# Token rows stored as they stand and gathered by quarters, q loaded two tokens to a partition, early gathers for two experts, the first weights loaded last

## The chip, the cores and the metric

The kernel runs on one core of one Trainium2 chip. The metric is device time in microseconds (us). Before the change three runs took 552.61, 552.60 and 547.84 us, so the median is 552.6 us. All line numbers below (L364 and so on) are those of the kernel before, unless the text says "after".

## The reference, cut to what matters

Two blocks follow each other: a retention layer (batch 4, 8 heads, 768 tokens, head width 64) and a mixture of experts over its output (3072 tokens of width 512, 8 experts, hidden width 1024, one expert for each token).

```python
for t in range(S):                      # retention, gamma per head
    state = gamma * state + einsum('bhd,bhe->bhde', k[:, :, t], v[:, :, t])
    y[:, :, t] = scale * einsum('bhd,bhde->bhe', q[:, :, t], state)
x = y.transpose(0, 2, 1, 3).reshape(B * S, H * D)          # 3072 x 512
logits = x @ w_gate
expert_idx = argmax(logits, axis=1)
gate_w = softmax(logits)[arange(N), expert_idx]
...
for e in range(E):
    h = maximum(x_sorted[lo:hi] @ w1[e], 0.0)
    y_sorted[lo:hi] = h @ w2[e]
out = gate_w[:, None] * y_sorted[inv_perm]
```

## The kernel before, in words

**Retention.** A chunk is 128 tokens of one batch; there are 6 chunks c times 4 batches b, so 24 steps n, in the order c outer, b inner. `load(n)` has SP fetch k, q and v of a step (256 KB each, rows of 64 floats), five steps ahead (`AHEAD`). `scale(n)` multiplies q and v by tables of decay powers on POOL. `transpose(n)` has PE turn k and q to heads-first form in PSUM and ACT copy them out (`kT`, L299, and `qT`, L300). `retain(n)` makes the scores (L311), masks them on DVE (`am`, L313), updates the state (L322, L325), and sums y (L335, L340), which ACT copies to `xTg` (L342). `to_rows` turns that into token rows `xg` on DVE (L347).

**Routing.** After the four batches of a chunk, `place(c)` runs in pieces, one at each `step()` of the following chunk, on all engines in an order written out by hand (`tc.manual_schedule`). It makes the logits, has ACT store `xg` in the DRAM tensor `x_d` (four DMAs, L364), finds expert, gate and rank of each token, stores the gate as column 513 of the row in `x_d` (L400), and adds the chunk's tokens to the table `inv` (slot to token) by the matmul `found` (L433). `tables` turns `inv` into row numbers: `src` to gather from `x_d`, `dst` to scatter to the output. SP is left to a scheduler; the DMAs of SP and ACT share eight completion semaphores in turn, and each waits for the DMA that had its semaphore before it.

**Experts.** Expert 0 begins early: at c = 4 `tables(inv[:, :, 0:HALF], "_e")` (L438) names its first 256 tokens, POOL gathers them (L159, one indirect DMA for 128 rows of 2052 bytes), and `layer1`/`layer2` run them between the pieces of the last `place`. Then `tables(inv)` (L507), the gathers of the rest, `turn` (gathered rows to features on partitions, 16 transposes of 32 partitions each, L191), and one `job` for each expert: 64 or fewer matmul groups of `layer1` (L200), then `layer2` (L212), gated on ACT (L218), scattered by POOL (L222). After job e POOL scatters its rows, and gathers those of e+2 (`rows_of`) while job e+1 runs; SP loads the weights of e+2 (L150, L151).

The lines of the indirect gather and of the store, which the change rewrites:

```python
R = DM + 1
x_d = dram.tile([N, R], F32, tag="x_d", name="x_d")
...
    nc.scalar.dma_start(x_d[ts(c, B * P), ts(g, P)].rearrange("(t l) r -> l t r", l=L),
                        xg[c % 2][ts(g, L), :, :, :].rearrange("p b q r -> p (b q) r"))
```

Of the kernel before, what the change touches and what calls it, by code (L numbers as in the profile page):

```python
# [20 lines left out]
P = 128  # L21


NC = 6


def decay_table(H, D):

    gamma = 1.0 - 2.0 ** (-5.0 - np.arange(H, dtype=np.float64))
    e = np.arange(1, P + 1, dtype=np.float64)[:, None]
    on = [gamma ** (e + P * c) / math.sqrt(D) for c in range(NC)]
    back = [gamma ** -(e + P * c) for c in range(NC)]
    return np.concatenate(on + back, 1).astype(np.float32)
# [15 lines left out]
def kernel(  # L53
# [39 lines left out]
    R = DM + 1  # L93
    x_d = dram.tile([N, R], F32, tag="x_d", name="x_d")

# [34 lines left out]
    tok2 = rt([P, NT, 2], "tok2", BF16)  # L130
# [3 lines left out]
    nc.gpsimd.iota(tok2[:, :, 0], pattern=[[1, NT]], base=1, channel_multiplier=0, **exact)  # L134
    nc.gpsimd.iota(tok2[:, :, 1], pattern=[[0, NT]], base=0, channel_multiplier=1, **exact)
# [3 lines left out]
    inv = rt([P, 2, E * TC], "inv")  # L139
# [15 lines left out]
    xs2 = [first.tile([P, TC, R], F32, tag=f"xs{i}", name=f"xs{i}") for i in range(2)]  # L155

    def gather(xs, idx, tiles, rows=N):
        for t in tiles:
            nc.gpsimd.indirect_dma_start(  # L159
                out=xs[:, t, :], out_offset=None, in_=x_d[0:rows, :],  # L160
                in_offset=bass.IndirectOffsetOnAxis(ap=idx[:, t : t + 1], axis=0), bounds_check=rows - 1,
                oob_is_err=False)

    def tables(got, name):

        m = got.shape[2]
        tok, none, far = (rt([P, m], f"{nm}{name}") for nm in ("tok", "none", "far"))
        src = rt([P, m], f"src{name}", U32)  # L170
        nc.vector.tensor_scalar(out=none, in0=got[:, 0, :], scalar1=1.0, scalar2=float(FAR), op0=ALU.is_lt,
                                op1=ALU.mult)
        nc.vector.scalar_tensor_tensor(out=tok, in0=got[:, 0, :], scalar=float(P), in1=got[:, 1, :], op0=ALU.mult,
                                       op1=ALU.add)
        nc.vector.scalar_tensor_tensor(out=src, in0=tok, scalar=-float(P), in1=none, op0=ALU.add, op1=ALU.add)
        tile_i, bt, ct = (rt([P, m], f"{nm}{name}", I32) for nm in ("tile_i", "bt", "ct"))
        dst = rt([P, m], f"dst{name}", U32)
        nc.vector.tensor_scalar(out=tile_i, in0=got[:, 0, :], scalar1=-1.0, scalar2=None, op0=ALU.add)  # L178
        nc.vector.tensor_single_scalar(bt, tile_i, B - 1, op=ALU.bitwise_and)
        nc.vector.tensor_single_scalar(ct, tile_i, B.bit_length() - 1, op=ALU.arith_shift_right)  # L180
        nc.vector.tensor_tensor(out=far, in0=got[:, 1, :], in1=none, op=ALU.add)
        nc.vector.scalar_tensor_tensor(out=far, in0=ct, scalar=float(P), in1=far, op0=ALU.mult, op1=ALU.add)
        nc.vector.scalar_tensor_tensor(out=dst, in0=bt, scalar=float(P * NC), in1=far, op0=ALU.mult, op1=ALU.add)
        return src, dst

    def turn(xs, xT, gate, tiles):

        nc.vector.tensor_copy(gate, xs[:, 0:tiles, DM])  # L188
        for r in range(Q):
            for g in range(Q):  # L190
                nc.vector.transpose(  # L191
                    xT[ts(g, L), :, 0 : tiles * P].rearrange("p a (t r i) -> p r t a i", r=Q, i=L)[:, r, :, :, :],
                    xs[ts(r, L), 0:tiles, ts(g, P)].rearrange("p t (a i) -> p t a i", i=L))
# [68 lines left out]
    with ExitStack() as actx:  # L262
# [5 lines left out]
        steps = [(c, b) for c in range(NC) for b in range(B)]  # L268
        qkv, scaled, front, state = {}, {}, {}, {}

        def load(n):
            c, b = steps[n]
            got = {}
            for nm, src in (("k", k), ("q", q), ("v", v)):
                got[nm] = att.tile([P, H, D], F32, tag=nm, name=nm, bufs=6)
                nc.sync.dma_start(got[nm], src[b, :, ts(c, P), :].rearrange("h t d -> t h d"))
            qkv[n] = got["q"], got["k"], got["v"]
# [7 lines left out]
        def scale(n):  # L285
            c, b = steps[n]
            qt, kt, vt = qkv.pop(n)
            mul = nc.gpsimd if n else nc.vector
            qs = att.tile([P, H, D], F32, tag="qs", name="qs", bufs=3)
            vs = att.tile([P, H, D], F32, tag="vs", name="vs", bufs=4)  # L290
            mul.tensor_tensor(out=qs, in0=qt, in1=inner(dec[:, ts(c, H)], D), op=ALU.mult)  # L291
            mul.tensor_tensor(out=vs, in0=vt, in1=inner(dec[:, ts(NC + c, H)], D), op=ALU.mult)  # L292
            scaled[n] = (qs, kt, vs)

        def transpose(n):
            qs, kt, vs = scaled.pop(n)
            qT = att.tile([P, HP, P], F32, tag="qT", name="qT")
            kT = att.tile([P, HP, P], F32, tag="kT", name="kT")
            nc.scalar.copy(out=kT, in_=heads_first(kt))  # L299
            nc.scalar.copy(out=qT, in_=heads_first(qs))  # L300
            front[n] = (kt, vs, qT, kT)

        def retain(n, then, between):
# [38 lines left out]
            nc.scalar.copy(out=xTg[c % 2][:, :, b, :], in_=y)  # L342

        def to_rows(n):

            c, b = steps[n]
            nc.vector.transpose(xg[c % 2][:, b, :, :].rearrange("p r (a l) -> p a r l", l=L),  # L347
                                xTg[c % 2][:, :, b, :].rearrange("p a (r l) -> p a r l", l=L))
# [3 lines left out]
        def place(c):  # L352
# [10 lines left out]
            for g in range(Q):  # L363
                nc.scalar.dma_start(x_d[ts(c, B * P), ts(g, P)].rearrange("(t l) r -> l t r", l=L),  # L364
                                    xg[c % 2][ts(g, L), :, :, :].rearrange("p b q r -> p (b q) r"))
# [33 lines left out]
            with nc.allow_non_contiguous_dma(reason="one gate a row"):  # L399
                nc.scalar.dma_start(x_d[ts(c, B * P), DM : DM + 1].rearrange("(b p) r -> p (b r)", p=P), gate)  # L400
# [17 lines left out]
            if c < NC - 1:  # L418
                yield
                yield  # L420
            val = att.tile([P, B, 2, E * TC], BF16, tag="val", name="val")
            at_f = at[:, :, :, :].rearrange("p b e t -> p b (e t)")
            nc.vector.tensor_tensor(out=val, op=ALU.mult, in1=inner(tok2[:, g0 : g0 + B, :], E * TC), in0=bass.AP(
                tensor=at_f.tensor, offset=at_f.offset,
                ap=[list(at_f.ap[0]), list(at_f.ap[1]), [0, 2], list(at_f.ap[2])]))
# [5 lines left out]
            found = ps("tr", 3, "found")[:, 0 : 2 * E * TC]  # L431
# [5 lines left out]
            if c == NC - 2:  # L437
                early.append(tables(inv[:, :, 0:HALF], "_e"))  # L438
                gather(xs2[0], early[0][0], range(HALF), (c + 1) * B * P)

                tot = ps("tr", 3, "tot")[:, 0:1]
                nc.tensor.matmul(tot, lhsT=ones_b, rhs=acc[:, c + 1, 0:1], start=True, stop=True)
                pad = att.tile([P, 1], F32, tag="pad", name="pad")
                nc.vector.scalar_tensor_tensor(out=pad, in0=row2, scalar=float(EARLY), in1=tot, op0=ALU.add,
                                               op1=ALU.subtract)
                nc.vector.tensor_scalar(out=pad, in0=pad, scalar1=0.0, scalar2=2.0, op0=ALU.max, op1=ALU.min)
                nc.vector.tensor_tensor(out=acc[:, c + 1, 0:1], in0=acc[:, c + 1, 0:1], in1=pad, op=ALU.add)
# [13 lines left out]
        for n in range(len(steps)):  # L461
            if n + AHEAD < len(steps):
                load(n + AHEAD)
            if n == 17:
# [18 lines left out]
            if steps[n][1] == B - 1:  # L483
                rest = place(steps[n][0])
        to_rows(len(steps) - 1)

        xe = keep.tile([P, HALF, DM], F32, tag="xe", name="xe")
        gates = [rt([P, HALF], "gate_e"), rt([P, TC - HALF], "gate_0")]
        for t in range(HALF):
            nc.vector.tensor_copy(xe[:, t, :].rearrange("p (a q l) -> p q a l", q=Q, l=L),  # L490
                                  xs2[0][:, t, 0:DM].rearrange("p (q a l) -> p q a l", q=Q, l=L))
        nc.vector.tensor_copy(gates[0], xs2[0][:, 0:HALF, DM])
# [3 lines left out]
        for t in range(HALF):  # L496
            tr = ps("tr", 3, "tre").rearrange("p (a t) -> p a t", a=DT)
            for dt in range(DT):
                nc.tensor.transpose(tr[:, dt, :], xe[:, t, ts(dt, P)], ident)
            nc.vector.tensor_copy(xTa[:, :, ts(t, P)], tr)  # L500
# [6 lines left out]
        src, dst = tables(inv, "")  # L507
        cols = [(src[:, ts(e, TC)], dst[:, ts(e, TC)]) for e in range(E)]

        cols[0] = tuple(t[:, HALF:] for t in cols[0])  # L510
        gather(xs2[1], cols[0][0], range(TC - HALF))
        turn(xs2[1], xTa, gates[1], TC - HALF)
        layer2(EARLY, hTa, wa[1], oa, 0, gates[0])
        which = regs(0)
        tc.switch_hint(which, arms_of(0), label="job0")
        layer2(EARLY, hTa, wa[1], oa, 1, gates[0])
# [10 lines left out]
    def job(e, n, xT, gate, hT, nxt):  # L527
# [5 lines left out]
        for t in [tiles - 1] + list(range(tiles - 1)):  # L533
            if e + 1 < E and t == max(tiles - 2, 0):
                tc.switch_hint({g: nxt[g] for g in (PE, ACT)}, arms_of(e + 1), label=f"job{e + 1}")
            layer2(n, hT, w2t, o2[e % 2], t, gate)
# [3 lines left out]
    def rows_of(e):  # L540

        xT = mp.tile([P, DT, W], F32, tag="xTs", name="xTs")
        xs = xs2[(e + 1) % 2]
        gather(xs, cols[e][0], range(TC))
# [115 lines left out]
```

## Time and profile before

The profiled execution took 544.2 us, of which its span is 542.5 us; the median of the three runs shown is 552.6 us.

| stretch of the span, us | what runs | PE busy in it, us |
|---|---|---|
| 0 to 16 | first loads and first step | 9.3 |
| 16 to 40 | chunk 0, start of chunk 1 | 23.8 |
| 40 to 108 | chunks 1 to 3 | 44.0 |
| 108 to 163 | chunks 3 to 5 | 53.2 |
| 163 to 205 | early half of expert 0, routing of chunk 5 | see below |
| 205 to 532 | eight expert jobs | 100% in all windows of 220 to 500 |

| engine | busy us, share of the span |
|---|---|
| PE | 490.7, 90% |
| DVE | 175.1, 32% |
| POOL | 119.0, 22% |
| ACT | 102.8, 19% |

Read the table of stretches first: the experts leave PE no idle time, the retention stage leaves it about 33 us in 163. DMA transfers are not engine work; the profile gives their bytes in each slice.

### The profile page before, as it was taken

The numbers are of one execution on the slowest core, as the hardware profiler recorded it, in microseconds if no ns is written. First come the engines' busy times: TensorE is split into PE (matmuls) and PEld (weight loads), VectorE is DVE, ScalarE is ACT, GpSimd is POOL, SyncE is SP. The second block draws the span as 40 slices with busy tenths as digits, with TensorE's granted clock in tenths as the row PEclk, the third lists the DMA queues.
The fourth block names the chain that finished last, engine by engine and source line by source line (L and its number), as shares of the span: only waits on it lengthen the run. The fifth ranks groups of instructions, "written<-read, shape, count | busy, mean of one in ns | idle before, by whom it ended". The sixth has DMA issues, their size and how long they took to land. (4 is left out here: it accounts for less than half of the span.)

```text
span 542.5 us, 7653 instructions
## 1 busy us (share of the span) xinstructions
PE 490.7 (90%) x3008; PEld 299.1 (55%) x3008; DVE 175.1 (32%) x405; ACT 102.8 (19%) x204; POOL 119.0 (22%) x135
## 2 busy tenths in 40 slices
PE   5997479299997978999999999999999999999991
PEld 4886368288774737555455455456455545445540
DVE  2565154246572549061025008003404300700000
ACT  2423022123331111022122021112002211111210
POOL 4825313033210050400230050023032004002010
PEclk9998869599997997999999999999999999999996
DMA  9999999999353691910660480075083057001010
GB/s 188 203 170 204 191 198 197 254 245 165 52 66 55 113 343 24 330 46 2 213 222 1 152 274 0 2 255 186 2 278 141 2 186 255 2 4 57 4 40 22
DMA packets 109143, 72.47 MB, mean 134 GB/s; under 512 B 81402, under 2 KB 93690, under 8 KB 109056
## 3 DMA queue, kind: packets, MB, share of 16 engines
q1 hardware_dynamic: 87952, 52.45, 39.5%
q10 hardware_dynamic: 15984, 6.35, 7.7%
q0 software_dynamic: 5120, 12.61, 6.2%
q8 instruction: 42, 0.69, 0.5%
q14 instruction: 45, 0.37, 0.2%
HBM read 60.90 MB, written 14.69 MB: 139 GB/s over the span
## 5 line engine op out<-in xcount | busy, mean ns | idle before, releaser
L212 PE MATMUL ye<-w2t,hT 128*128 128x512 f32 (+3 forms) x640 | 164.0, 455 | 0.0
L200 PE MATMUL hp<-xTs,w1t 128*128 128x416 f32 (+3 forms) x448 | 154.2, 505 | 0.0
L200 PEld LDWEIGHTS hp<-xTs,w1t 128*128 128x128 f32 x448 | 85.1, 190 | 69.1 <-issue 54.6
L212 PEld LDWEIGHTS ye<-w2t,hT 128*128 128x128 f32 (+3 forms) x640 | 74.9, 155 | 86.5 <-issue 85.0
L222 POOL DMA_INDIRECT out_dram<-o,dst x30 | 29.9, 996 | 269.0 <-ACT o L218 236.6
L191 DVE STREAM_TRANSPOSE xTs<-xs 32x512 f32<-32x512 f32 x112 | 78.7, 702 | 1.4
L188 DVE COPY gates<-xs 128x4 f32<-128x4 f32 x7 | 1.2, 170 | 185.4 <-DMA xs<-x_d,src 185.4
L202 ACT ACTIVATE hT<-hp 128x416 f32<-128x416 f32 (+4 forms) x64 | 29.4, 482 | 136.3 <-PE hp L200 93.1
L313 DVE TENSOR_TENSOR am<-sc,causal 128x512 f32<-128x512 f32 x48 | 30.8, 683 | 35.1 <-PE sc L311 32.2
L159 POOL DMA_INDIRECT xs<-x_d,src x30 | 30.3, 1011 | 37.3 <-DVE tile_i L178 28.4
L218 ACT ACTIVATE o<-ye,gates 128x512 f32<-128x512 f32 (+1 forms) x21 | 14.5, 689 | 125.5 <-PE ye L212 125.5
L322 PE MATMUL new<-vs,k 128*64 128x64 f32 x320 | 15.5, 247 | 21.8 <-ACT kT L299 21.8
L292 POOL TENSOR_TENSOR vs<-v,dec 128x512 f32<-128x512 f32 x23 | 24.1, 1048 | 48.3 <-PE y L340 38.2
L311 PE MATMUL sc<-qT,kT 64*128 64x128 f32 x384 | 29.4, 295 | 4.3 <-ACT qT L300 4.3
L291 POOL TENSOR_TENSOR qs<-q,dec 128x512 f32<-128x512 f32 x23 | 24.0, 1042 | 40.2 <-DMA q<-in_q_dram 23.3
L200 PE MATMUL hp<-xTa,w1t 128*128 128x256 f32 (+1 forms) x128 | 26.5, 373 | 6.2 <-DVE xTa L191 4.8
L342 ACT COPY xTg<-y 128x512 f32<-128x512 f32 x24 | 14.1, 588 | 84.7 <-PE y L340 35.6
L311 PEld LDWEIGHTS sc<-qT,kT 64*128 64x128 f32 x384 | 24.7, 197 | 8.2 <-ACT qT L300 5.2
L340 PE MATMUL y<-am,vs 128*64 128x128 f32 x384 | 29.2, 292 | 0.0
L200 PEld LDWEIGHTS hp<-xTa,w1t 128*128 128x128 f32 x128 | 22.2, 224 | 10.9 <-issue 7.3
L322 PEld LDWEIGHTS new<-vs,k 128*64 128x64 f32 x320 | 12.5, 154 | 27.4 <-ACT kT L299 22.6
L340 PEld LDWEIGHTS y<-am,vs 128*64 128x64 f32 x384 | 22.7, 145 | 4.1 <-issue 2.4
(121 smaller groups left out, 282.3 us busy)
## 6 DMA issues: line engine op xcount, KB each, us to landing
w1t<-in_moe_w_dram SPq DMA_DIRECT2D x8, 2048.0 KB, 9.3
w2t<-in_moe_w_dram SPq DMA_DIRECT2D x8, 2048.0 KB
k<-in_k_dram SPq DMA_DIRECT2D x24, 256.0 KB, 6.0
q<-in_q_dram SPq DMA_DIRECT2D x24, 256.0 KB, 6.4
v<-in_v_dram SPq DMA_DIRECT2D x24, 256.0 KB, 6.6
x_d<-xg ACTq DMA_DIRECT2D x24, 256.0 KB, 8.9
xs<-x_d,src POOLq DMA_INDIRECT x30
out_dram<-o,dst POOLq DMA_INDIRECT x30
```

What stands on the lines that cost most here:

```text
L159: nc.gpsimd.indirect_dma_start(out=xs[:, t, :], out_offset=None, in_=x_d[0:rows, :], in_offset=bass.IndirectOffsetOnAxis(ap=idx[:, t : t + ...
L191: nc.vector.transpose(xT[ts(g, L), :, 0 : tiles * P].rearrange("p a (t r i) -> p r t a i", r=Q, i=L)[:, r, :, :, :], xs[ts(r, L), 0:tiles, ...
L200: nc.tensor.matmul(hp, lhsT=w1t[:, 0, dt, ts(f, P)], rhs=xT[:, dt, 0:n], start=(dt == 0), stop=(dt == DT - 1))
L202: nc.scalar.activation(out=hT[:, f, 0:n], in_=hp, func=AF.Relu)
L212: nc.tensor.matmul(y[j * m : j * m + m, 0:c], lhsT=hT[:, f, t * P : t * P + m], rhs=w2t[:, 0, f, ts(j, c)], start=(f == 0), stop=(f == FT ...
L222: done = nc.gpsimd.indirect_dma_start(out=out[:, :], out_offset=bass.IndirectOffsetOnAxis(ap=idx[:, t : t + 1], axis=0), in_=o[:, t, :], i ...
L291: mul.tensor_tensor(out=qs, in0=qt, in1=inner(dec[:, ts(c, H)], D), op=ALU.mult)
L292: mul.tensor_tensor(out=vs, in0=vt, in1=inner(dec[:, ts(NC + c, H)], D), op=ALU.mult)
L311: nc.tensor.matmul(sc[j][:, a, :], lhsT=kT[r, a, :], rhs=qT[r, a, :], start=True, stop=True)
L313: nc.vector.tensor_tensor(out=am[j], in0=sc[j], in1=middle(causal[:, :], HP), op=ALU.mult)
L322: nc.tensor.matmul(new[ts(j, D), a, :], lhsT=kt[:, h, :], rhs=vs[:, h, :], start=True, stop=True)
L340: nc.tensor.matmul(y[ts(j, D), a, :], lhsT=vs[:, 2 * a + j, :], rhs=am[j][:, a, :], start=(c == 0), stop=True, skip_group_check=True)
```

## The change

1. **Layout of x_d.** It becomes 12288 rows of 128 floats (a quarter of a token each), and each chunk group is stored in one DMA of 1 MB, partition after partition, as `xg` stands. The gate is stored no more: it travels through `inv` as three bf16 parts, so `inv`, `val` and `found` have 5 planes for 2.
2. **Gather.** An indirect DMA now fetches the four quarters of 32 tokens (128 rows of 512 bytes), so an expert takes 16 for 4. `tables` spreads the token numbers over the quarters with four small matmuls (`ip`, with the constant `wrap`). `turn` becomes 4 transposes of 128 partitions.
3. **Order of steps.** Steps run in pairs of chunks: for each pair m, for each batch, the two chunks. q is loaded once for a pair, two tokens to a partition (512-byte rows), scaled and transposed in the even step; `qT` interleaves the tokens again. A group for `place` is four consecutive steps, thus 2 batches by 2 chunks.
4. **Early gathers** for experts 0 and 1 (256 tokens each); the early compute stays with expert 0, and no `xe` copies or transposes on PE are made for it.
5. **First weights.** They are asked for at n = 19, no longer at n = 17.

```diff
-    x_d = dram.tile([N, R], F32, tag="x_d", name="x_d")
+    x_d = dram.tile([N * Q, DT * L], F32, tag="x_d", name="x_d")
...
+        hl = rt([P, 2, m], f"hl{name}", BF16)
+        nc.vector.tensor_copy(hl, got[:, 0:2, :])
+        ip = ps("tr", 3, "ip")[:, 0 : Q * 2 * m].rearrange("p (g i m) -> p g i m", g=Q, i=2)
+        for g in range(Q):
+            nc.tensor.matmul(ip[:, g, :, :].rearrange("p i m -> p (i m)"), lhsT=wrap[:, g, :],
+                             rhs=hl[:, :, :].rearrange("p i m -> p (i m)"), start=True, stop=True)
...
+    def turn(xs, xT, b0, b1):
+
+        for dt in range(DT):
+            nc.vector.transpose(xT[:, dt, :], xs[:, b0:b1, ts(dt, L)])
...
-        steps = [(c, b) for c in range(NC) for b in range(B)]
+        steps = [(2 * m + e, b) for m in range(NC // 2) for b in range(B) for e in range(2)]
...
+                elif c % 2 == 0:
+                    got[nm] = att.tile([P, H, 2 * D], F32, tag=nm, name=nm, bufs=3)
+                    nc.sync.dma_start(got[nm], src[b, :, ts(c // 2, 2 * P), :].rearrange("h (t e) d -> t h (e d)", e=2))
...
+                qT2[b] = att.tile([P, HP, P, 2], F32, tag="qT", name="qT")
+                for e in range(2):
+                    nc.scalar.copy(out=qT2[b][:, :, :, e], in_=heads_first(qs[:, e, :, :]))
...
-            for g in range(Q):
-                nc.scalar.dma_start(x_d[ts(c, B * P), ts(g, P)].rearrange("(t l) r -> l t r", l=L),
-                                    xg[c % 2][ts(g, L), :, :, :].rearrange("p b q r -> p (b q) r"))
+            nc.scalar.dma_start(x_d[ts(c, B * P * Q), :].rearrange("(p r) d -> p r d", p=P),
+                                xg[c % 2][:, :, :, :].rearrange("p b r d -> p (b r) d"))
...
-                nc.scalar.dma_start(x_d[ts(c, B * P), DM : DM + 1].rearrange("(b p) r -> p (b r)", p=P), gate)
...
+            part = gate
+            for i in range(2, 5):
+                nc.vector.tensor_copy(told[:, g0 : g0 + B, i], part)
+                if i < 4:
+                    less = att.tile([P, B], F32, tag="less", name="less", bufs=3)
+                    nc.vector.tensor_tensor(out=less, in0=part, in1=told[:, g0 : g0 + B, i], op=ALU.subtract)
+                    part = less
...
-                gather(xs2[0], early[0][0], range(HALF), (c + 1) * B * P)
+                for e in range(2):
+                    gather(xs2[e], early[0][0][:, e * TC * Q :],
+                           range(HALF * Q), (c + 1) * B * P * Q)
...
-            if n == 17:
+            if n == len(steps) - AHEAD:
                 wa = weights(first, 0)
...
-        for t in range(HALF):
-            tr = ps("tr", 3, "tre").rearrange("p (a t) -> p a t", a=DT)
-            for dt in range(DT):
-                nc.tensor.transpose(tr[:, dt, :], xe[:, t, ts(dt, P)], ident)
-            nc.vector.tensor_copy(xTa[:, :, ts(t, P)], tr)
+        turn(xs2[0], xTa, 0, HALF * Q)
...
+        for e in range(2):
+            gather(xs2[e], cols[e][0], range(HALF * Q, TC * Q))
+        turn(xs2[0], xTa, HALF * Q, TC * Q)
```

## The prediction

> **What bounds the kernel now.** I began with the slices of the page, to see which stage leaves PE idle.
>
> ```profile
> PE   5997479299997978999999999999999999999991
> DMA  9999999999353691910660480075083057001010
> GB/s 188 203 170 204 191 198 197 254 245 165 52 66 55 113 343 24 330 46 2 213 222 1 152 274 0 2 255 186 2 278 141 2 186 255 2 4 57 4 40 22
> ```
>
> From slice 16 on PE is full: the experts are bound by PE, and nothing there gets shorter, as the change leaves their matmuls alone. The first 12 slices (163 us) have holes in PE while DMA is full. The table by stretches says where (length, then busy us of PE, PEld, DVE, ACT, POOL, granted clock, DMA share, GB/s):
>
> ```profile
> 40.00:48.00 8.00, 5.10 (x64) 4.44 (x60) 3.86 (x9) 2.58 (x5) 3.27 (x3) 0.88 0.91 176
> 60.00:72.00 12.00, 1.50 (x26) 1.38 (x24) 1.34 (x5) 1.68 (x4) 3.12 (x3) 0.63 1.13 183
> 92.00:108.00 16.00, 5.60 (x69) 5.17 (x67) 3.78 (x15) 1.68 (x4) 2.08 (x2) 0.67 1.22 235
> ```
>
> Three holes, of 2.9, 10.5 and 10.4 us. The wait list names one releaser for PE (total, times, longest), and the timeline of ACT, then that of all engines, shows what held that releaser (start, length, engine and line):
>
> ```profile
> PE new L322 <- ACT kT L299: 21.8, 7, 10.5
> ```
>
> ```profile
> 89.75 14.71 ACTq L364 DMA_DIRECT2D x_d<-xg  x4
> 104.50 0.59 ACT L342 COPY xTg<-y 128x512 f32<-128x512 f32 x1 [14.39 <-DMA v<-in_v_dram]
> ...
> 105.11 0.58 ACT L299 COPY kT<-tr 128x512 f32<-128x512 f32 x1
> ```
>
> ```profile
> 105.74 1.12 PE L322 MATMUL new<-vs,k 128*64 128x64 f32 x16 [10.40 <-ACT kT L299]
> ```
>
> ACT is no slow engine (19% busy): it stands for 14.7 us inside the issue of four stores to x_d, since each waits for the completion semaphore of an earlier load. The copies of kT and xTg queue behind, and PE behind them. So two things act together: loads that keep DMA full, and a store of four DMAs (plus one for the gate) that ties ACT to the progress of those loads four times a chunk.
>
> [...] with k, q and v alone in flight 218 GB/s move (8 to 16 us), with weights, whose rows are 2 to 4 KB, 362 GB/s (192 to 196 us). [...] SP's issues stretch from 1.1 to 5.4 us when the stores run (33.8 us). [...] the granted clock is 0.50 in the windows of 68 to 76 and 100 to 108.
>
> **The change part by part.** Sums are against the profiled execution (span 542.5, device time 544.2).
>
> *Stores of x_d.* ACT's queue has 6.35 MB in 7.7% of 16 engines' span:
>
> ```profile
> q1 hardware_dynamic: 87952, 52.45, 39.5%
> q10 hardware_dynamic: 15984, 6.35, 7.7%
> ```
>
> That is 0.077 x 542.5 = 41.8 us of all engines, 7.0 us a chunk, 152 GB/s. Stored as 8 KB a partition at the weights' 362 GB/s a chunk takes 2.9; five chunks lie in the loaded stretch, so 20 us of DMA go. Lower bound 0, if stores are slow whatever their rows. The gate's 4-byte rows go with it.
>
> *q by 512 bytes.* 6.29 MB take 28.8 us at 218 GB/s; [...] Bounds 0 and 11; I take 5.
>
> *What that buys.* Loads and stores keep DMA full to about 131 us. Less 25 they need 106, for 24 steps 4.4 us a step, while PE works 5.14 a step where nothing holds it (138.5 to 143.6). DMA ceases to be the bound. ACT now waits for a semaphore once a chunk, not five times; in the built order that is a load for two to five steps ahead, which has landed once loads run ahead. Of the holes' 23.8 us I take 22.3 as gone, and 1.5 left. Late next is PE's own work.
>
> *Clock.* After each long hole PE does 38 to 41 matmul records in 4 us at a clock of 0.50 to 0.63, for 62 at full clock. Two such ramps of about 2 us: -4.
>
> *Start.* Step 0 needs 1 MB for 0.75 MB, then two multiplications by 0.69 on DVE and 8 transposes of q for 4: +1.5, and POOL's `wrap` is hidden behind the loads (POOL idle 5.5 us before 9.28). Step 1 needs no q; bounds 0 and 3.
>
> *Scaling, transposes, copies of q.* As many as before in total (POOL 1.04, ACT 0.59 each), three in even steps and one in odd. POOL has 3.1 us of 5.1 in an even step. Nothing, if PE stays the slowest.
>
> *Routing on DVE.* Five more operations of 0.17 a chunk, `val` 640 wide for 256 (0.4 to about 0.8), `found` 160 columns for 64. DVE is busy for 11.9 of 20 us (120 to 140), so this is covered, save in chunk 4: there `tables` stands right before the mask `am` of step 22, which before ended only 0.1 us before its matmul needed it (157.40 against 157.30). About 10 more operations of 0.16, plus 0.85, 0.4, and PE waiting for `ip`: +3.0.
>
> *Early gathers.* Before, 2; now 8 for expert 0 (and 8 for expert 1 behind them). One costs POOL 1.3, start to start:
>
> ```profile
> 273.08 1.04 POOL L159 DMA_INDIRECT xs<-x_d,src  x1 [0.30 <-issue]
> 274.43 1.01 POOL L159 DMA_INDIRECT xs<-x_d,src  x1 [0.31 <-issue]
> 275.74 1.00 POOL L159 DMA_INDIRECT xs<-x_d,src  x1 [0.30 <-issue]
> 277.04 1.00 POOL L159 DMA_INDIRECT xs<-x_d,src  x1 [0.31 <-issue]
> ```
>
> Their data is there 3.3 us after the last (DVE goes on at 281.32). I hold the cost to follow the 128 rows, not their length; the scatters of 2048-byte rows (1.0) can't tell, so bounds are 0.8 and 2.6. Before, they began 3.4 us ahead of the end of attention (162.8), waiting for the four stores and the gate issued from 145.8 on; with one store they wait for `src_e` alone, some 10 us ahead. So 8 x 1.3 + 3.3 - 10 = 3.7 after the end, then 4 transposes of about 0.44: PE begins 5.3 after the end, before 3.9 (166.69): +1.3. The PE transposes of `xe` go within that.
>
> *Second gathers.* Expert 0's rest: 8 for 2, so 6 x 1.3 = 7.8 later; 16 transposes (7.2 us, 198.1 to 205.3) become 4 (1.8): 5.4 sooner. Weights of expert 1 moved in the same stretch and delayed the two gathers (issued 192.75, read 197.98); now the gathers end after them: 2 sooner. Longer tables: +1.3. Two memsets of `o` (1.76 each) stand before the `inv` sum on DVE in the built order where they stood amid the tables before, and no longer wait for the gate's store (3.2 us, 186.1): -2.6 in all. Together -0.9, bounds -4 and +6.
>
> *Experts.* After each job POOL has 4 scatters and 16 gathers, 26 us, then 3.3 and 4 x 0.70 = 32 us, against jobs of 39.5 to 48.5 us from the starts of L200 (shortest 360.17 to 399.70). Cover is 7 us: nothing. Before, 10.4 + 3.3 + 11.4.
>
> *First weights.* Two DMAs of SP, now ahead of 5 loads in the built order (before 10). Issue near 105, 11.5 us to move, wanted at about 145; cover about 25 us. Nothing.
>
> Sum: -22.3 - 4 + 1.5 + 3.0 + 1.3 - 0.9 = -21.4. Span 521.1, device 522.8 for 544.2. The median shown is 8.4 above the profiled execution; I take the gain off the median: 552.6 - 21.4 = **531.2**.
>
> **The rivals.**
>
> *DMA stays the bound.* Stores gain half (10 us), q nothing, and ACT still stands one long wait a chunk. For it: DMA is full in all slices to 9, and no trace shows these row shapes. Against it: four waits in a row made the 14.7. Holes give back 11 for 22: 541.
>
> *POOL becomes the bound (slower).* A gather costs more than 1.3, say by contention with the weights' rows. Place: POOL's queue between the scatters of e and the transposes for e+2. With g a gather, 4 x 1.3 + 16 g + 6.1 must fit the job; it costs from g = 1.75 in the shortest job. At 2.1 (44.9 us) jobs 4 and 6 lose 5.4 and 3.7 and the junctions 8 x 0.8 = 6.4 each: 22 us, which uses up the gain, so the sign turns there. At 2.2 six jobs lose 17 and the junctions 14: 562. At the bound 2.6, 52.9 for 44 on average, 53 us over six jobs and 21 at the junctions: 605. Against it: 30 gathers measure 997 to 1052 ns at any load.
>
> *The change doesn't do what it says.* Stalls go, but the work shifted to the end of attention (tables, 16 gathers before PE can go on) eats them: 549 to 557.
>
> **How the numbers follow.** Main case 0.66, own range 520 to 539 (bounds of start, tables, second gathers, and 0 to 6 us of holes left); DMA stays 0.17, 535 to 547; POOL 0.11; eaten 0.06. Over 1% faster is under 547.1; within 1% is about what a measurement can tell here, the three runs spread by 0.9%. Faster: 0.66 + 0.16 = 0.82; same: 0.01 + 0.06 + 0.01 = 0.08; slower: 0.10. The range 519 to 545 leaves out the last two rivals and the tails.
>
> **What would show it.** Right: no wait of PE for kT over 3 us; the store one issue of ACT of under 2 us; ACT's queue about 3% of 16 engines; attention ends near 140; expert jobs as long as before, DVE waiting for gathers without PE waiting for DVE. Wrong: PE waiting for xTs in the jobs (POOL), or ACT still standing at the store (DMA). A gather's issue far from 1.3 us, or stores not faster by bytes, overturns the sum.

## The result, and the profile after

| | kernel before | changed kernel |
|---|---|---|
| median of the runs | 551.99 us (4 runs, 547.84 to 552.61) | 568.59 us (4 runs, 566.72 to 571.05) |
| profiled execution / its span | 544.2 / 542.5 us | 566.72 / 565.0 us |

The ratio is 1.032, with a 95% interval of 1.025 to 1.039: slower, where 531.2 us was forecast. One thing has to be said at once, since no number below can be read without it: this kernel has two times. In two sets of runs (this one and a later one) it took 567 to 569 us; in two others, the same file took 517 us. I call the first sets disturbed and the others undisturbed. What separates them lies outside the kernel, and finding that out took most of the experiments. This section reads the disturbed trace that belongs to the result.

The slices of the changed kernel (busy tenths of PE and of DMA, and GB/s, in 40 slices of 14.1 us):

```profile
PE   5998999996189959989969999999998899799992
DMA  9999999911117118104610650192371047101010
GB/s 207 224 238 233 240 263 274 271 75 27 48 75 281 54 50 317 43 2 151 235 33 2 196 199 13 46 323 56 111 254 38 2 152 240 32 5 55 1 41 21
```

The holes that PE had in the first slices are gone up to slice 9, and DMA is full for 8 slices, to 113 us, where it was full for 10, to 136. But there is a new hole in slices 10 to 12, and PE, full before from slice 16 to the end, now has fives to eights among the jobs. The queues of SP and ACT (packets, MB, share of 16 engines):

```profile
q1 hardware_dynamic: 75472, 52.45, 34.4%
...
q10 hardware_dynamic: 1008, 6.34, 3.0%
```

ACT's stores take 0.030 x 565 = 17 us of all engines for 41.8. The timeline of ACT at the fourth store (start, length, engine and line) shows one issue of 0.33 us; before, ACT stood 14.7 us in the issue of the four DMAs of one store (89.75, 90.77, 94.97 and 104.15, each 0.02 to 0.08 us after the recorded landing of a load with the same semaphore; that trace has eight semaphores on the 120 DMAs of SP and ACT):

```profile
99.74 0.58 ACT L410 COPY lgT<-parts 128x512 f32<-128x512 f32 x1 [0.38 <-PE parts L407]
100.06 0.33 ACTq L411 DMA_DIRECT2D x_d<-xg  x1
```

PE's longest wait for kT is 0.7 us. The first half of the change does what it says. The loss comes after 130 us. The table by stretches (length, then busy us of PE, PEld, DVE, ACT, POOL, granted clock, DMA share, GB/s):

```profile
100.00:120.00 20.00, 20.00 (x279) 16.59 (x277) 13.92 (x43) 7.33 (x14) 6.82 (x7) 1.00 0.60 184
136.00:142.00 6.00, 2.84 (x44) 2.30 (x40) 0.51 (x2) 0.58 (x1) 4.49 (x5) 0.93 0.19 51
146.00:156.00 10.00, 0.15 (x1) 0.00 (x0) 0.00 (x0) 0.39 (x1) 5.90 (x6) 0.50 0.17 46
```

In the ten us from 146 on nothing works but POOL. The timeline of all engines there:

```profile
145.91 1.00 POOL L174 DMA_INDIRECT xs<-x_d,src_e  x1 [0.30 <-issue]
...
152.42 1.00 POOL L174 DMA_INDIRECT xs<-x_d,src_e  x1 [0.30 <-issue]
155.61 0.58 ACT L390 COPY xTg<-y 128x512 f32<-128x512 f32 x1 [16.59 <-remote]
156.23 0.71 DVE L395 STREAM_TRANSPOSE xg<-xTg 128x512 f32<-128x512 f32 x1 [11.49 <-ACT xTg L390]
...
157.37 1.19 PE L235 MATMUL hp<-xTa,w1t 128*128 128x256 f32 x2 [11.22 <-issue]
```

The last matmul of `y` ended, by its modelled end, at 146.15. ACT's copy of that `y` (L390) waited 16.6 us and began at 155.61; "remote" is a wait that was ended by a semaphore whose update came much later than the instruction that makes it. The trace's record of PE's semaphore has that update at 155.59, 9.4 us late and 2.2 us after POOL's sixteenth early gather had ended (153.42). The updates of ACT and DVE have their records 0.01 us after the instruction in the median. So PE's work, or the news of it, was held up while POOL issued gathers, although DMA moved only 46 GB/s.

The same happens in the jobs. The timeline of ACT in job 1:

```profile
233.43 0.52 ACT L237 ACTIVATE hT<-hp 128x416 f32<-128x416 f32 x1 [2.28 <-PE hp L235]
237.21 0.52 ACT L237 ACTIVATE hT<-hp 128x416 f32<-128x416 f32 x1 [3.26 <-PE hp L235]
242.16 0.52 ACT L237 ACTIVATE hT<-hp 128x416 f32<-128x416 f32 x1 [4.43 <-remote]
245.55 1.10 ACT L251 COPY o<-ye 32x128 f32<-32x128 f32 x4 [2.88 <-PE ye L247]
```

PE hands over a block of `hp` every 2.80 us; then come 3.8, 4.95 and 3.4, where 2.8 and 1.9 are usual. POOL's run of 2 scatters and 16 gathers goes from 218.1 to 241.3, so it is the end of the run that hurts (in the undisturbed trace of the same file, below, ACT gets its blocks of `hp` 2.79 to 2.80 us apart to the end of the layer). Lengths of the jobs, from the first matmul of `hp` in one to that in the next:

| us | early layer 1 begins | to job 0 | job 0 | 1 | 2 | 3 | 4 | 5 | 6 | 7 |
|---|---|---|---|---|---|---|---|---|---|---|
| before | 166.7 | 38.7 | 16.3 | 45.0 | 45.0 | 48.5 | 39.5 | 45.0 | 41.2 | 45.2 |
| changed, this trace | 157.4 | 35.0 | 24.1 | 50.4 | 53.7 | 49.9 | 39.9 | 54.2 | 44.7 | 45.2 |
| changed, undisturbed (below) | 145.1 | 34.6 | 15.2 | 45.1 | 45.0 | 48.5 | 40.0 | 45.0 | 41.2 | 45.2 |

9.3 and 3.7 us are won up to job 0, 7.8 lost in it and 28.6 in jobs 1 to 6. Job 7, in which no gathers run, loses nothing. Jobs 3 and 4 have a run of 20 indirect DMAs each and lose only 1.4 and 0.4 us, so the length of the run alone doesn't set the loss.

### The profile page after: what moved, and what is told of

It reads as the page before. It is cut to its first block, busy times and chain, and to the rows that moved or that the text cites. A ratio compares the mean times of both kernels' runs of the same rounds, so it can differ in the third digit from the quotient of the medians.

```text
span 565.0 us, 7708 instructions
## 1 busy us (share of the span) xinstructions
PE 501.0 (89%) x3008; PEld 300.6 (53%) x3008; DVE 124.2 (22%) x356; ACT 104.3 (18%) x204; POOL 215.1 (38%) x232
## 5 line engine op out<-in xcount | busy, mean ns | idle before, releaser
L247 PE MATMUL ye<-w2t,hT 128*128 128x512 f32 (+3 forms) x640 | 175.9, 481 | 16.4 <-issue 13.1
L235 PE MATMUL hp<-xTs,w1t 128*128 128x416 f32 (+3 forms) x448 | 154.4, 505 | 0.1
L247 PEld LDWEIGHTS ye<-w2t,hT 128*128 128x128 f32 (+3 forms) x640 | 79.6, 164 | 110.0 <-issue 104.6
L174 POOL DMA_INDIRECT xs<-x_d,src x112 | 111.9, 999 | 60.8 <-issue 33.8
L235 PEld LDWEIGHTS hp<-xTs,w1t 128*128 128x128 f32 x448 | 85.0, 190 | 69.6 <-issue 54.3
L228 DVE STREAM_TRANSPOSE xTs<-xs 128x512 f32<-128x512 f32 x28 | 17.4, 680 | 284.8 <-DMA xs<-x_d,src 233.3
L335 POOL TENSOR_TENSOR vs<-v,dec 128x512 f32<-128x512 f32 x23 | 25.3, 1102 | 55.0 <-DMA v<-in_v_dram 17.0
L235 PE MATMUL hp<-xTa,w1t 128*128 128x256 f32 (+1 forms) x128 | 27.5, 378 | 19.2 <-issue 11.2
L253 ACT ACTIVATE o<-ye,gate 128x512 f32<-128x512 f32 (+1 forms) x22 | 15.1, 687 | 125.8 <-PE ye L247 120.4
L235 PEld LDWEIGHTS hp<-xTa,w1t 128*128 128x128 f32 x128 | 22.7, 225 | 23.9 <-issue 14.0
L359 PEld LDWEIGHTS sc<-qT,kT 64*128 64x128 f32 x384 | 24.1, 193 | 4.9 <-issue 2.7
L390 ACT COPY xTg<-y 128x512 f32<-128x512 f32 x24 | 14.1, 586 | 66.0 <-PE y L388 44.6
L332 POOL TENSOR_TENSOR qs<-q,dec 128x512 f32<-128x512 f32 x22 | 22.5, 1043 | 7.7 <-DMA q<-in_q_dram 7.4
L174 POOL DMA_INDIRECT xs<-x_d,src_e x16 | 16.2, 1014 | 18.7 <-DVE at_e L210 14.2
L383 PE MATMUL y<-qT,state 64*64 64x128 f32 x320 | 21.8, 275 | 0.0
L321 PE MATMUL tr<-ident,k 128*128 128x128 f32 x96 | 16.2, 292 | 4.5 <-DMA k<-in_k_dram 4.5
```

Of the source, the lines that this page charges most:

```text
L174: nc.gpsimd.indirect_dma_start(out=xs[:, b, :], out_offset=None, in_=x_d[0:rows, :], in_offset=bass.IndirectOffsetOnAxis(ap=idx[:, b : b + ...
L228: nc.vector.transpose(xT[:, dt, :], xs[:, b0:b1, ts(dt, L)])
L235: nc.tensor.matmul(hp, lhsT=w1t[:, 0, dt, ts(f, P)], rhs=xT[:, dt, 0:n], start=(dt == 0), stop=(dt == DT - 1))
L247: nc.tensor.matmul(y[j * m : j * m + m, 0:c], lhsT=hT[:, f, t * P : t * P + m], rhs=w2t[:, 0, f, ts(j, c)], start=(f == 0), stop=(f == FT ...
L332: mul.tensor_tensor(out=qs[:, e, :, :], in0=got["q"][:, :, ts(e, D)], in1=inner(dec[:, ts(c + e, H)], D), op=ALU.mult)
L335: mul.tensor_tensor(out=vs, in0=got["v"], in1=inner(dec[:, ts(NC + c, H)], D), op=ALU.mult)
```

## Experiments

Six sets of runs, each on one chip, with the kernel before in each. The line numbers and names are those of the changed kernel, where nothing else is said. Sets 1 to 3 were run first and sets 4 to 6 after them. split4, no_gather, paced, pool_busy, pause1, early8, early8_2 and plain16 are single executions, the others medians of four.

| set | kernel before, median | run with it |
|---|---|---|
| 1 (the result) | 552.0 | the changed kernel 568.6 |
| 2 | 540.6 | split4 571.4, no_gather 540.6, paced 548.2, rows2k 529.0 |
| 3 | 541.9 | pad516 523.2, pool_busy 538.3, sp_store 517.7, after_again 567.4 |
| 4 (the chip of set 3) | 541.3 | pad_sp 520.6, pad514 525.4, pause1 516.7, early8 528.1 |
| 5 | 549.2 | after_3 516.9, pause1_2 516.7, early8_2 528.0 |
| 6 | 550.3 | after_4 517.1, plain16 517.5, sp_store_2 516.0 |

### Is it the number of gathers?

Three theories for the loss, A, B and C, are set out in what I expected of split4. It is the kernel before with only the gathers of experts 1 to 7 split (and x_d padded to R = 516, so that a row falls into four equal parts):

```diff
-        gather(xs, cols[e][0], range(TC))
+        for t in range(TC):
+            for g in range(Q):
+                nc.gpsimd.indirect_dma_start(
+                    out=xs[:, t, ts(g, R // Q)], out_offset=None,
+                    in_=x_d[:, :].rearrange("n (j r) -> (n j) r", j=Q),
+                    in_offset=bass.IndirectOffsetOnAxis(ap=src4[:, e * TC + t, g : g + 1], axis=0), ...)
```

> The kernel before, with each row of x_d (padded from 513 to 516 floats) fetched in four pieces of 129, so that an expert takes 16 gathers for 4 and the bytes stay. Theory A (a run of indirect DMAs that POOL issues without a pause leaves PE about 100 more matmuls and weight loads, and after that one in 0.35 us until some 2 us past the run): jobs 1 to 6 lose what they lost in the changed kernel, 5.4, 8.7, 1.4, 0.4, 9.3 and 3.4 us, and job 0 some 5 to 8: 29 to 37 us over the kernel before. Theory B (PE and ACT wait for results or buffers of POOL, whose queue is too long): POOL has 26 us of work for jobs of 39 us and more, so 0 to 3 us. Theory C (the bytes of the gathers and the weights contend): the bytes are the same, so -2 to +3 us.

Measured: 571.43 us. Jobs 0 to 6 took 26.4, 50.9, 54.4, 51.5, 47.1, 53.0 and 46.6: 10.1 and 39.3 us over the kernel before, where theory A said 29 to 37 in all. B doesn't give it: PE has no wait for `xTs`, the transposed rows. The bytes are the same, which speaks against C; the pieces gathered are four times as many, and that was not tried apart from the number of gathers. PE's waits in this kernel (line numbers of the kernel before):

```profile
PE ye L212 <- issue: 19.2, 16, 4.3
PE new L322 <- ACT kT L299: 11.5, 7, 6.6
PE hp L200 <- ACT hT L202: 10.7, 1, 10.7
```

The first and third line are the ones that the changed kernel has, too (13.1 and 6.8 us there). The second has halved without any edit aimed at it; pad516 follows it up.

no_gather takes the gathers of experts 2 to 7 out of the changed kernel:

```diff
-        if e > 1:
+        if e > 1 and e < 0:
             gather(xs2[e % 2], cols[e][0], range(TC * Q))
```

> The changed kernel, without the gathers of experts 2 to 7 (their rows are left out, the old ones of xs are turned again). Theory A, and C too: jobs 1 to 6 are as long as before the change (45.0, 45.0, 48.5, 39.5, 45.0, 41.2 us), 28 us less than the changed kernel, some 538 us; job 0 keeps its 24 us, as its gathers stay. If the jobs stay longer than before the change, the loss has to do with the transposes, the weights or the code, not with the gathers.

Measured: 540.55 us, jobs 1 to 6 of 45.0, 45.0, 48.5, 39.5, 45.0 and 41.2, job 0 of 26.4, and early layer 1 at 157.0. The gathers, not the transposes or the code, make the 28 us; where they stayed, at the end of attention and in job 0, the loss stayed.

pool_busy puts 32 memsets into their place:

```diff
-            gather(xs2[e % 2], cols[e][0], range(TC * Q))
+            for _ in range(TC * Q * 2):
+                nc.gpsimd.memset(idle, 0.0)
```

> The changed kernel, without the gathers of experts 2 to 7 (their rows are left out) and with 32 memsets of about 0.5 us on POOL in the place of each expert's 16 gathers. Theory A (a run of indirect DMAs starves PE): POOL's being busy does nothing, jobs 1 to 6 as without gathers (45.0, 45.0, 48.5, 39.5, 45.0, 41.2 us), some 540 us. If it is POOL's work of any kind, or its queue being long: jobs 1 to 6 as in the changed kernel, some 28 us longer, 565 us.

Measured: 538.25 us, the same lengths of jobs 1 to 6, in a set in which the changed kernel itself took 567.36. The memsets keep POOL busy for 32 x 0.526 = 16.8 us, the gathers for 20.8. POOL's being busy did nothing to PE in this run.

paced keeps all gathers and breaks up the runs:

```diff
-            gather(xs2[e % 2], cols[e][0], range(TC * Q))
+            for t in range(TC):
+                gather(xs2[e % 2], cols[e][0], range(t * Q, (t + 1) * Q))
+                if t < TC - 1:
+                    for _ in range(5):
+                        nc.gpsimd.memset(idle, 0.0)
```

> The changed kernel with the 16 gathers of experts 2 to 7 in groups of four, and five memsets (about 2.5 us in all) on POOL between the groups. Theory A: no run is longer than 8 indirect DMAs, PE gets through it with its 100 instructions if 2.5 us are enough to begin anew: jobs 1 to 6 near the lengths before the change, 20 to 28 us less than the changed kernel. If the pause is too short, less than 5 us change. Theory B: POOL is 7.5 us later each time: 0 to 10 us slower. Theory C: the same bytes in 28 us for 21: 0 to 5 us less.

Measured: 548.24 us; jobs 1 to 6 of 47.0, 47.0, 48.5, 42.1, 46.9 and 41.2, 8.5 us lost for 28.6. The gain of theory A came, at its lower end. In set 2, then, it was POOL's indirect DMAs in close order (one every 1.30 us) that held PE up. Whether a pause helps because it ends a run or because it makes gathers fewer per us, paced can't tell; pause1, below, was to do that, but came into an undisturbed set.

rows2k keeps the retention of the changed kernel (q by pairs, early gathers for two experts, gates from the tables) and goes back to 4 gathers an expert; x_d is [N, DM], the turn is that of the kernel before, and the store is four DMAs again:

```diff
-    x_d = dram.tile([N * Q, DT * L], F32, tag="x_d", name="x_d")
+    x_d = dram.tile([N, DM], F32, tag="x_d", name="x_d")
...
-            nc.scalar.dma_start(x_d[ts(c, B * P * Q), :].rearrange("(p r) d -> p r d", p=P),
-                                xg[c % 2][:, :, :, :].rearrange("p b r d -> p (b r) d"))
+            for g in range(Q):
+                nc.scalar.dma_start(x_d[ts(c, B * P), ts(g, P)].rearrange("(t l) r -> l t r", l=L),
+                                    xg[c % 2][ts(g, L), :, :, :].rearrange("p b q r -> p (b q) r"))
```

> The changed kernel with x_d stored as whole rows of 2 KB (four DMAs for one, 512 bytes a piece, the gate not stored) and fetched by 4 gathers an expert, turned by 16 transposes as before the change; q by two tokens, early gathers for two experts and the late first weights stay. Theory A: the jobs are as long as before the change, the retention keeps most of its gain: 524 to 535 us, 4% faster than the kernel before. If the gain of the retention came from the store as one DMA, the holes at the store come back: 540 to 548. Theories B and C: the jobs are as before the change too.

Measured: 528.98 us, ratio 0.977 (0.969 to 0.985), within the range expected in us, though 2.3% faster for 4. Jobs 1 to 6 are those of the kernel before. ACT stands 7.8 us in the issue of one store, and waits of PE behind kT come to 9.3 us.

### What of the store was slow?

pad516 is the kernel before with rows of 2064 bytes for 2052:

```diff
-    R = DM + 1
+    R = DM + 4
...
-                nc.scalar.dma_start(x_d[ts(c, B * P), DM : DM + 1].rearrange("(b p) r -> p (b r)", p=P), gate)
+                nc.scalar.dma_start(x_d[ts(c, B * P), DM:R].rearrange("(b p) r -> p b r", p=P), gate4)
```

> The kernel before with rows of x_d of 516 floats for 513 (2064 bytes for 2052, the gate written four times), nothing else. In the run with split gathers, which had this padding too, ACT's queue took 4.7% of 16 engines' span (26.8 us) for 41.8 us, a store landed in 5.5 us for 8.9, and PE waited 11.5 us for kT for 21.8. If the padding did that: 4.7 to 5% here, and 525 to 537 us, 2 to 3% faster than the kernel before. If it was the shift of the gathers or chance: as the kernel before, within 1%.

Measured: 523.18 us, ratio 0.966 (0.961 to 0.971). Three floats a row are worth 18.7 us here, where the whole change was to bring 21.4. Its queue of ACT, and PE's wait (line numbers of the kernel before):

```profile
q10 hardware_dynamic: 15984, 6.39, 5.3%
```

```profile
PE new L322 <- ACT kT L299: 9.7, 8, 5.5
```

As many packets as before the change, 15984, in 0.053 x 521.4 = 27.6 us for 41.8; a store lands 5.8 us after its issue for 8.9.

> The kernel before with rows of x_d of 514 floats (2056 bytes), the gate written twice. If what counts is that rows begin on multiples of 16 bytes: as the kernel before, store queue near 7.7% of 16 engines, 536 to 544 us. If 4-byte pieces, or rows off by 4 bytes, are what was slow: as with 516 floats, 5.3%, 521 to 527 us.

pad514, with R = DM + 2, took 525.37 us, 0.968 (0.961 to 0.975), with 5.9% for that queue (31 us). So it isn't multiples of 16 bytes that count; a pitch of 2056 does nearly as well as 2064.

The gate's rows grew from 4 to 8 and 16 bytes with the pitch, and no run tried the two apart, but the traces' records of single packets do. The 512-byte pieces of xg alone took 38.0 us of all engines before, 28.9 at 2056 and 25.2 at 2064; the 4-byte packets, gates among them, took 3.6 before, and the gates' own packets 1.9 and 1.7 in the two. So the pieces make 12.8 of the 14.2 us. The loads beside them gain as much: the 256-byte packets of k, q and v, which nobody changed, took 113.4 us before and 96.9 in pad516. Why 2052 is slow stays open.

sp_store is rows2k with the four stores issued by SP:

```diff
-                nc.scalar.dma_start(x_d[ts(c, B * P), ts(g, P)].rearrange("(t l) r -> l t r", l=L),
+                nc.sync.dma_start(x_d[ts(c, B * P), ts(g, P)].rearrange("(t l) r -> l t r", l=L),
```

> The kernel with rows of 2 KB and 4 gathers an expert, its four stores of x_d issued by SP for ACT. If ACT's standing in the issue of the stores is what is left of the holes (7.8 us at 85, 21 us of waits of xTg): PE waits for kT under 3 us, early layer 1 starts 6 to 10 us sooner, 518 to 524 us. If SP stands in its place and holds back the loads behind the stores: DMA under 9 tenths in the slices to 100 us, PE waits for loads of k, 528 to 538 us.

Measured: 517.65 us, ratio 0.955 (0.950 to 0.960). PE's longest wait for kT is 0.7 us, early layer 1 begins at 144.2 for 157.5. The slices of PE and DMA:

```profile
PE   4998999999789799999999999999999999999991
DMA  9999989798235529006602810480480084010010
```

DMA does fall below nine in slices 6, 8 and 10, as the rival said, but PE has its loads all the same (its one wait for a load in this trace is of 4.4 us). Its comparison with rows2k is one across sets 2 and 3; the kernel before took 540.6 and 541.9 us in them.

> The kernel before with rows of x_d of 516 floats and its four stores issued by SP for ACT; q, gathers and early expert as before. If ACT's standing in the issue makes the 9.7 us of waits for kT that the padded kernel has left: those go, 513 to 518 us, 0.95 times the kernel before. If SP holds back the loads in its place (q is loaded by 256 bytes here, so DMA is busier than in the kernel with pairs): 519 to 526 us.

pad_sp, the kernel before with R = DM + 4 and the stores on SP, took 520.61 us, 0.963 (0.958 to 0.968): of the 9.7 us of waits 0.9 are left, but only 2.6 us of time came of it against pad516 (the two stand in different sets). That is the range of the rival. Early layer 1 begins at 149.7 for 149.1, so the retention won nothing: PE waits for loads of k instead, 8.4 us for 4.7 in pad516.

```profile
PE tr L282 <- DMA k<-in_k_dram: 8.4, 2, 4.4
```

### The theory falls, and what takes its place

> The changed kernel as it is, on the same chip as the others: 1.032 times the kernel before (1.025 to 1.039), its jobs 0 to 6 longer by 36 us in sum than those of the kernel before.

after_again, the changed kernel in set 3: 567.36 us, ratio 1.048 (1.042 to 1.053), jobs 0 to 6 longer by 39 us. So far all agrees with theory A. Then set 4:

> The changed kernel with the gathers of experts 2 to 7 in groups of four, and one memset of 0.5 us between the groups for five. Theory A in the form that a pause of any length begins anew: as with five memsets, 548 us (0.966 of the changed kernel). In the form that PE gets its instructions at the pauses' rate (about 0.35 us each, when DMAs run): no gain worth the name, 558 to 566 us. Between: 550 to 558.

> The changed kernel with early gathers for expert 0 alone: a run of 8 at the end of attention for 16, the 8 of expert 1 put into the second run, 24 for 16. Theory A: PE comes free some 2 us after the eighth gather, near 145, and early layer 1 begins at 146 to 149 for 156.4; the second run, 31 us, begins 8 us sooner and ends about where it did, so job 0 begins at 184 to 188 and has its 26 us or up to 8 more. Without theory A (early layer 1 waited for its own data, which POOL brings first): the 8 gathers of expert 1 behind them don't matter, begins at 156 again.

pause1 is paced with `range(1)` for `range(5)`: 516.65 us. early8 gathers early for expert 0 alone:

```diff
-                for e in range(2):
-                    gather(xs2[e], early[0][0][:, e * TC * Q :],
-                           range(HALF * Q), (c + 1) * B * P * Q)
+                gather(xs2[0], early[0][0], range(HALF * Q), (c + 1) * B * P * Q)
...
-            gather(xs2[e], cols[e][0], range(HALF * Q, TC * Q))
+            gather(xs2[e], cols[e][0], range(0 if e else HALF * Q, TC * Q))
```

It took 528.05 us. Both misfit. early8 has a run of 44 indirect DMAs without a pause (167 to 224) and its jobs 2 to 6 have runs of 19 or 20, as in the changed kernel; yet those jobs take 45.0, 48.5, 39.6, 45.0 and 41.2. pause1 has the changed kernel's run of 16 at the end of attention, word for word, and early layer 1 begins at 144.8 for 156.4. (Job 0 of early8 takes 24.5 us, since expert 1's rows come late from POOL and PE waits for them: `PE hp L235 <- DVE xTs L228: 10.0, 1, 10.0`. That is where its 11 us over the changed kernel of set 5 go, and what gathering early for expert 1 is worth in an undisturbed set.) Theory A in its plain form, that a long run starves PE, is wrong: it does so in some sets only. I had no changed kernel in set 4 to compare with, so set 5 has one:

> The changed kernel as it is. If the program decides whether runs of gathers hold PE up: 564 to 571 us as twice before, jobs 0 to 6 longer by 36 us than those of the kernel before, while the two kernels beside it are at 517 and 528. If it is something outside the program (call it theory E): all three are disturbed or none is; undisturbed, the changed kernel takes 513 to 522 us, with jobs of 45.0, 45.0, 48.5, 39.5, 45.0, 41.2 us and no completion of PE over 1 us late.

> The kernel with one memset of 0.5 us between groups of four gathers, once more. If the program decides: 517 us again. Theory E, disturbed: early layer 1 begins at 156 for 144.8, as in the changed kernel, whose code it shares up to there, and the jobs lose 8 to 30 us in sum: 540 to 562. Theory E, undisturbed: 517.

> The kernel with early gathers for expert 0 alone, once more. If the program decides: 528 us again, no job from 2 on longer than before the change. Theory E, disturbed: jobs 1 to 6 lose some 28 us with their runs of 20, 550 to 560. Theory E, undisturbed: 528.

after_3, the changed kernel: 516.87 us, ratio 0.942 (0.938 to 0.945). pause1_2 516.74, early8_2 528.01. Theory E holds: all three were undisturbed, and the pause of pause1 is worth nothing there. The slices of the changed kernel in set 5, and two stretches for those shown of set 1:

```profile
PE   4998999999869999999999999999999999999991
DMA  9999999962135448106513810471471084001010
```

```profile
136.00:142.00 6.00, 4.36 (x64) 3.42 (x60) 2.92 (x5) 1.17 (x2) 4.47 (x6) 1.00 0.16 45
146.00:156.00 10.00, 9.40 (x48) 6.78 (x48) 2.82 (x17) 1.97 (x5) 5.71 (x6) 0.86 0.43 152
```

POOL issues the same run of 16 gathers (132.4 to 153.2), at the same 1.30 us each, and PE works beside it. No wait in this trace is "remote".

The traces have one more mark of the sets, the increments of semaphores that they record for DMAs. Up to 130 us every trace of the changed kernel has 1104, 16 for each of 69 DMAs. From there on, where the indirect ones begin, there are 175 DMAs, and sets 5 and 6 have 2795 and 2798 (16 each would be 2800); sets 1 and 3 have 841 and 819. The waits are met, so the increments did arrive, and it is their records that are missing. Of PE's completions, 57 in set 1 and 61 in set 3 have no record within 1 us after them (some come late, of some only the record is missing); in the traces of sets 4 to 6 none.

The mark divides all traces alike. In set 2 no_gather has 1916 of 2368 increments and paced 2611 of 3904, so set 2 was disturbed; in set 4 pause1 has 3897 and early8 3904 of 3904. And the profiled execution of the kernel before, in set 1, has 2463 of 2944, and sp_store in set 3 has 2176 of 2656, though PE is full in their jobs. So a disturbed set loses records whatever the kernel, and costs time only in the kernels that gather a row in four pieces: on the chip of sets 3 and 4 the kernel before took 541.9 us in the disturbed set and 541.3 in the other. It isn't the chip as such, since sets 3 and 4 ran on the same one, nor the kernel; the three sets that were run first are disturbed and the three after them are not. What changed between them no run shows. Nor does any show whether the recording has a part in it, as every timed execution here was a recorded one.

The last set was to tell whether plain DMAs do the same. plain16 has, for each 16 gathers in the jobs,

```diff
+            for b in range(TC * Q):
+                nc.sync.dma_start(xs2[e % 2][:, b, :], x_d[ts(b, P), :])
```

> The changed kernel once more, as the mark of the set. In a disturbed set 564 to 571 us and fewer than 900 increments of DMAs recorded after 130 us; in an undisturbed one 515 to 519 us and some 2800.

> The changed kernel with 16 plain loads of 128 rows of 512 bytes by SP in the place of each 16 gathers of experts 2 to 7 (other rows than the experts' own are computed with). Undisturbed set: jobs 1 to 6 as before the change, 515 to 520 us. Disturbed set: if the number of DMAs and increments holds PE up, jobs 1 to 6 lose up to 28 us, 555 to 570 us; if only POOL's indirect DMAs do, they lose nothing, 536 to 542 us, as without gathers.

The mark came out undisturbed (after_4 517.14 us, ratio 0.940, 0.932 to 0.947), so plain16 with its 517.52 us tells nothing on that: inconclusive. In the same set:

> The kernel with rows of 2 KB, 4 gathers an expert and stores of x_d by SP once more. In a disturbed set 517 us as before, 50 us less than the changed kernel. Undisturbed: 514 to 518 us, within 1% of the changed kernel, as neither has holes in the retention and both have PE full in the jobs.

sp_store took 516.04 us, 0.940 (0.932 to 0.947). It is the version to keep: level with the changed kernel in an undisturbed set, and 50 us ahead of it in set 3, where both were run.

## Why the prediction was wrong, point by point

*The step that failed* is "Experts": "Cover is 7 us: nothing", and the same under "Early gathers", where 16 of them were priced at 1.3 us of POOL's time each. I counted what a gather takes from POOL (1.0 + 0.30 us, which held in all traces: 1.01 us on average for 128 rows of 2052 bytes before, 1.00 for 128 of 512 in set 1) and nothing of what a run of them can do to PE. In set 1 that was 12.3 us at the end of attention (157.4 for 145.1), 8.9 in job 0 and 28.0 in jobs 1 to 6, 49.2 of the 49.7 us between the traces of sets 1 and 5. The rival that had POOL as the bound named the place, and its 562 comes near the time by luck: it has a dearer gather, and the gather was not dearer. PE itself was held up, with POOL on time. Why it is held up in some sets only stays open; in the undisturbed ones the term held, with 264.8 us for jobs 1 to 6 where the kernel before has 264.2.

*Stores.* 2.9 us a chunk were forecast, 17 / 6 = 2.8 measured. The reason given, the length of a row, was half the truth: by pad516, 14 of the 25 us that went are had with the old 512-byte pieces and another pitch (with the gate's wider rows). I read 152 GB/s off the page and took piece length as its cause.

*q.* SP's queue took 214 us of all engines before (39.5%), 192 in set 5 (37.3% of 515.3); pad516, whose q is the old one, is at 197. That leaves some 4 us for q, near the 5 taken, which was an estimate of mine between 0 and the 11 that rows moving at the weights' 362 GB/s would give, and rested on no trace of such rows; the other 17 went in pad516 too, so they came with the faster stores, and the prediction has no term for them.

*Holes, clock, start, tables.* Right as a sum: -22.3, -4, +1.5 and +3.0 make -21.8, and undisturbed the last `y` of attention ends at 140.4 for 162.8, so -22.4; the four weren't measured apart. *Early gathers.* +1.3 forecast: early layer 1 begins 4.7 us after that for 3.9, so +0.8, undisturbed. *Second gathers.* -0.9 forecast; from early layer 1 to job 1, 49.8 us undisturbed for 55.0 before, so -5.2, outside the bound of -4. *First weights.* Nothing, right: PE waits for none.

*The sum* against the span was -21.4; undisturbed it is 542.5 - 515.3 = 27.2, disturbed +22.5. So undisturbed the sum was 5.8 us short, 4.3 of it in the second gathers, and it was out by 44 in the set that counts. The range could have held that only with a rival in which the added gathers slow another engine. The kernel before showed no loss of this kind: in its job 2, while POOL issued 4 scatters and 4 gathers, PE was full. The missing records were there in its trace, but say nothing of PE by themselves.

## What to carry to other kernels

A gather had the price that POOL paid here, 1.30 us, and in set 1 a second one, what its runs did to PE, 49.2 us in all; if a change multiplies one kind of instruction by four and makes runs of 20 out of runs of 8, test that alone before trusting a row of the old profile. Before explaining a loss, run the same file again in another set: here a theory stood through eight runs of sets 2 and 3, and fell when the same file, run later, took 50 us less. Look at the pitch of a DRAM array before rebuilding around it: three floats of padding gave 0.966 of the time where the rebuilt layout gave 0.94 or 1.05.

## What the runs showed of the hardware that was not expected

- In the disturbed trace of set 1 PE gets through much the same number of matmuls and weight loads after a run of indirect DMAs begins, and then falls behind. The first block that ACT gets over 1 us later than in the undisturbed trace is the one with the 87th to 103rd of them in seven of the eight long runs (in job 5 it comes after the 101st), whether that is 4.1 us into the run (small matmuls of attention) or 14 to 20 (the expert layers). Near the end of the run in job 1 single matmuls of layer 2 stand 0.70 us apart (240.03, 240.72, 241.42, 242.13); undisturbed, four of them start every 0.11 us. A count, not a time or a number of gathers, would explain that; what it counts is open.
- The stores of 512-byte pieces took 41.8 us of all DMA engines at a pitch of 2052 bytes, 31 at 2056 and 27.6 at 2064, each with its gates; without gates and at 2048, 25.4 (rows2k, 4.8% of 528.9). The pieces alone: 38.0, 28.9, 25.2 and 24.9.
- DMA at one to two tenths and POOL's gathers on time said nothing of PE: in the stretch of 146 to 156 us of set 1 DMA had a share of 0.17 (46 GB/s), POOL issued a gather every 1.30 us up to 153.42, PE was busy for 0.15 us, and no wait pointed at POOL.
